# Retention attention and top-1 experts on one core: where the table read, found rows, decayed queries, weight pieces and first loads stand in the program order

## The chip, the cores and the metric

The kernel runs on one core of a Trainium2 chip. The metric is device time in microseconds (us), the median of three runs; three runs of the kernel before took 421.93, 422.62 and 422.92 us, so its time is 422.62 us.

## The reference

Block-wise retention attention (B = 4, H = 8, S = 768, D = 64, blocks of 64) yields x, 3072 rows of 512. A top-1 mixture of 8 experts follows:

```python
logits = x @ w_gate
e_idx = np.argmax(logits, axis=1)
...
for e in range(E):
    mask = e_idx == e
    h = np.maximum(x[mask] @ w1[e], 0.0)
    ye = h @ w2[e]
    out[mask] = gate_w[mask, None] * eom[mask, e, None] * ye
```

Here `gate_w` is the winning probability and `eom` a sigmoid of a second gate. All of it is float32; w1 is 512 x 1024 and w2 is 1024 x 512 for each expert.

## The kernel before, in words

**Attention.** x is made in 24 tiles of 128 rows (`NTILE`). A loop over s = -2 to 21 runs, for each s, `stage_a(s + 2)` (turning keys and queries: psum banks `pk`, `pq`), `stage_c1(s)` (the queries times the running state, into `po`), `stage_b(s + 1)` (keys times queries: `ps`), `stage_b2(s + 1)` (VectorE: `at` = `ps` times the decay table, L396) and `stage_c(s)` (`at` times values, L431, and the copy to `xT`). `decay_queries(n)` (L356) makes the decayed queries `qd` that `stage_c1(n)` reads; for tile 23 the tile is named `qkv_23_1`. `RES` is 16.

**Routing of the first expert ahead of time.** The routes of tiles 0 to 15 (`x_d` holds their rows in DRAM, `store_x` L521) are known before attention ends. `place_scatter` (L697) writes (row, gate) records to the table `tab_d`; `load_rows` (L822) reads an expert's part of it back as `index`; `row_index` (L846, L851) turns that into gather indices `rows`. For expert 0, rows found by a matmul (`pfound`) are added: `row_join` transposes them on VectorE (`found`, L865) and adds (L869). `gather` (L887, GpSimd, an indirect DMA of one 32-row group into `xg`) then fetches rows of x: eight gathers, here called [0] to [7], fill `xg_0_0` and `xg_0_1`, two in each of the steps s = 18 to 21. `pace` (L839, `beat`) makes GpSimd wait for a tile of the attention before the second of each pair. `x_turn(0, 0)` and `x_turn(0, 1)` (VectorE, L904) transpose the two halves into `y_0_0`; `fill` then runs expert 0's first products on TensorE (`ph` from `y` and `raw`, L938) in between the last routing steps. They are the first work of the experts that TensorE can do.

**Experts.** Weights come in 1 MB pieces, four for each expert (`load_piece`, L112, tile `raw`): pieces 0 and 1 are w1 of expert 0, 2 and 3 its w2, 4 and 5 are w1 of expert 1, 6 and 7 its w2. ScalarE and VectorE split each into two parts (`whi`, `wlo`), and a product is three matmuls (L79 to L81); their left side is split into `xhi` (ScalarE, L918) and `xlo` (VectorE, L922). Expert 1's rows are gathered as [0] to [13]: ten behind the read of its indices, the last four during expert 0's second half of rows. `next_split` splits a piece by quarters and loads the one two further on.

**What sets the order.** All of this stands in one hand-written program order (`manual_schedule`): every engine runs its own instructions in that order. SyncE (SP), ScalarE and GpSimd (POOL) issue DMAs, each in its own order. A DMA also waits for the one that stands eight before it among the DMAs of its kind (hardware queues of SP and ScalarE, software queue of POOL), here called its lane. The start loads keys and queries of tiles 0 to 4 and values of 0 to 2 (L200 to L205), then the loop goes on tile by tile; the gate weights `wgs` come over ScalarE's queue at L1237.

Of the kernel before, what the change touches and what calls it, by code (L numbers as in the profile page):

```python
# [23 lines left out]
def kernel(  # L24
# [13 lines left out]
    nc = tc.nc  # L38
# [140 lines left out]
    with tc.manual_schedule():  # L179
# [22 lines left out]
        for n in range(2, AHEAD):  # L202
            load_qkv(n, 0, 2)
            if n > 2:
                load_qkv(n - 2, 2, 3)  # L205
    kdec = const.tile([P, H, 1], F32, name="kdec")
# [151 lines left out]
    def stage_a2(n):  # L358
        c, b = divmod(n, B)
        L = live[n]  # L360
        if c > 0:
            qd = packs[n][3] if n in packs else slot(f"qd_{n}")
            L["qd"] = qd.rearrange("p (g t) -> p g t", g=NPAIR)
            if n not in (RES + 5, RES + 6):
                decay_queries(n)
        weave()
        weave()
        if c < NCH - 1:
            L["kd"] = slot(f"kd_{n}").rearrange("p (h d) -> p h d", h=H)
# [491 lines left out]

    def row_join(j0, pf, width):
        nb = width // 32
        turned = slot(f"found_{j0}")
        nc.vector.transpose(turned[:, 0:width], pf[:, 0:width])  # L865
        gi = const.tile([P, nb], I32, name=f"rows0_{j0}")
# [300 lines left out]
    with tc.manual_schedule():  # L1167
# [12 lines left out]
        for s in range(-2, NTILE - 2):  # L1180
# [19 lines left out]
            if s == RES + 2:  # L1200
                pfound = bank("pfound")
                for b in range(B):
                    found(pfound, RES - B + b, 0, 2 * P, b == 0, b == B - 1)
                row_index(0)
                row_join(0, pfound, 2 * P)
            n = s - 1
# [4 lines left out]
            if n >= 0 and n % B == B - 1:  # L1211
                at_once(route_choose(n + 1 - B, n + 1))
                if n < RES:
                    pace(routed[n + 1 - B][0][0:1, 0, 0:1])
                else:
                    decay_queries(s + 2)
                ranking = route_place(n + 1 - B, n + 1)
                per_turn[0] = 3 if n >= RES - 1 else 2
            stage_k(s + 2)
            if s == RES + 1:  # L1220
# [14 lines left out]
            if s == 1:  # L1235
                weave(len(later))
                nc.scalar.dma_start(wgs[:, :, 0:E], w_gate.rearrange("(c p) e -> p c e", p=P))  # L1237
                nc.scalar.dma_start(wgs[:, :, E : 2 * E], w_output_gate.rearrange("(c p) e -> p c e", p=P))
            if s == 2:
                blank_rows()  # L1240
# [17 lines left out]
            if s >= RES + 2:  # L1258
                pace(xTs[s][0:1, 0:1])
                gather(0, 2 * (s - RES - 2) + 1, 2 * (s - RES - 2) + 2, RES * P)  # L1260
                if s < RES + 4:
                    place_scatter(1)
                if s == RES + 4:
                    load_rows(0, 2, None, nc.gpsimd)
            if s == RES + 5:
                load_piece(1)
            if s < RES:
                place_scatter(1 if s < RES - 2 else 2)

        load_piece(2)  # L1270
        n = NTILE - 1
# [21 lines left out]
        x_turn(0, 1)  # L1293
        stage_d2(n - 3, 2)
        fill(3)
        for f in place[1:]:
# [23 lines left out]
        place_scatter(len(pending))  # L1320
        fill(5)
        row_index(0, 2)
        row_join(2, pfound, late_width)
        gather(0, 8)
# [4 lines left out]
        load_piece(4, nc.gpsimd)  # L1329
        load_piece(5, nc.gpsimd)  # L1330
        load_outs(0)
# [5 lines left out]
        for j in range(4):  # L1337
            split_quarter(3, j)
            if j == 3:
                row_index(1)  # L1340
                gather(1, 0, 10)
            fill(2)
            settle()
# [13 lines left out]

        def next_split(i, quarters):
            for qq in quarters:
                split_quarter(i + qq // 4, qq % 4)  # L1360
                if qq % 4 == 3:
                    load_piece(i + 2 + qq // 4)

        for p in range(E):
# [5 lines left out]
            for fc in range(NFC):  # L1370
                if p == 0:
                    up(p, fc, 1)
                    if fc >= 4:
                        next_split(4, (fc - 4,))
                        for f in work[:2]:
# [211 lines left out]
```

## Time and profile before

| | us |
|---|---|
| three runs | 421.93, 422.62, 422.92 |
| the profiled execution | 423.13 |
| its span in the trace | 421.1 |
| TensorE busy in the span | 401.2 (95%) |
| VectorE busy | 279.1 (66%) |
| ScalarE busy | 183.4 (44%) |
| GpSimd busy | 234.1 (56%) |

The profiled execution is one run by itself; 2.0 us of it lie outside the span that the trace records. The views used are the busy time in windows of the span, the waits of an engine with what released them, the timeline of one engine (start, duration, idle time ahead of it and the releaser), and the view of one source line with the times from issue to landing of its DMAs. A releaser is inferred; where the engine that it names was long done, it was another wait.

### The profile page before, as it was taken

How to read it: one execution, taken by the hardware profiler on the slowest of the kernel's cores; microseconds unless marked ns; L12 is line 12 of the kernel's file. 1: busy time of each engine (PE TensorE's matmuls, PEld its weight loads, DVE VectorE, ACT ScalarE, POOL GpSimd, SP SyncE). 2: the span in 40 equal slices, each digit the busy share in tenths (PEclk: the TensorE clock that was granted, in tenths of full speed). 3: DMA queues.
4: the chain of work that ended last, by engine and by line, in shares of the span. 5: the costliest groups of instructions: out<-in, count | busy, mean ns of one | idle time of the engine just before them, and what ended most of it. 6: DMA issues, size and time to landing. Idle time of an engine off the chain costs nothing.

```text
span 421.1 us, 10323 instructions
## 1 busy us (share of the span) xinstructions
PE 401.2 (95%) x3775; PEld 366.6 (87%) x3775; DVE 279.1 (66%) x789; ACT 183.4 (44%) x449; POOL 234.1 (56%) x306
## 2 busy tenths in 40 slices
PE   7899999998849999999999999999999999999995
PEld 4789889787638898699999999999999989988985
DVE  3858778676847826586778957966885774864511
ACT  3667666685412414445325504704632542551500
POOL 2468876935665768487575557466286356302002
PEclk9999999998979999999999999999999999999999
DMA  9987988999935383355367747936965866462001
GB/s 183 215 200 181 232 226 226 272 269 234 352 121 175 65 318 112 98 196 169 127 189 225 260 161 208 304 132 183 297 211 150 292 237 206 131 188 84 0 26 48
DMA packets 101861, 78.98 MB, mean 188 GB/s; under 512 B 66348, under 2 KB 78128, under 8 KB 101808
## 3 DMA queue, kind: packets, MB, share of 16 engines
q1 hardware_dynamic: 92736, 62.80, 52.2%
q0 software_dynamic: 6816, 15.19, 11.4%
q8 instruction: 31, 0.51, 0.5%
q10 hardware_dynamic: 2256, 0.30, 0.5%
q14 instruction: 22, 0.18, 0.1%
HBM read 62.45 MB, written 16.21 MB: 187 GB/s over the span
## 4 chain that ended last, share of the span: by engine, by line
PE 78%; DMA 9%; DVE 4%; SPq 3%; issue 3%; ACT 1%; POOL 1%; POOLq 0%; ACTq 0%; DVEq 0%
PE ph_None L80 10%; PE ph_None L81 10%; PE ph_None L79 9%; PE py L79 6%; PE py L80 6%; PE py L81 6%; DMA xg<-x_d,rows 5%; PE pyr L81 4%; PE pyr L80 4%; PE pyr L79 4%; PE ph L938 4%; PE ps L387 3%; PE po L431 3%; DMA qkv<-in_q_dram 2%; PE po L411 2%
## 5 line engine op out<-in xcount | busy, mean ns | idle before, releaser
L887 POOL DMA_INDIRECT xg<-x_d,rows x103 | 113.6, 1103 | 65.8 <-issue 30.7
L134 DVE TENSOR_TENSOR wlo<-raw,whi 128x512 fp32r<-128x512 f32 x120 | 79.6, 685 | 0.8 <-ACT whi L125 0.5
L964 ACT ACTIVATE hhi<-ph_None 128x400 fp32r<-128x400 f32 (+4 forms) x56 | 28.0, 501 | 114.4 <-PE ph_None L81 108.2
L79 PE MATMUL ph_None<-xhi,whi 128*128 128x400 f32 (+4 forms) x224 | 76.5, 342 | 0.7 <-ACT xhi L918 0.7
L80 PE MATMUL ph_None<-xlo,whi 128*128 128x400 f32 (+4 forms) x224 | 76.5, 342 | 0.3 <-DVE xlo L922 0.3
L81 PE MATMUL ph_None<-xhi,wlo 128*128 128x400 f32 (+4 forms) x224 | 76.4, 341 | 0.0
L125 ACT CAST whi<-raw 128x512 fp32r<-128x512 f32 x120 | 69.9, 614 | 0.0
L965 DVE SCALAR_TENSOR_TENSOR hlo<-ph_None,hhi 128x400 fp32r<-128x400 f32 (+4 forms) x56 | 31.7, 567 | 34.1 <-ACT hhi L964 33.8
L396 DVE TENSOR_TENSOR at<-ps,decay 128x512 f32<-128x512 f32 x48 | 31.3, 685 | 21.6 <-PE ps L387 21.5
L79 PE MATMUL py<-hhi,whi 128*128 128x400 f32 (+2 forms) x128 | 44.7, 349 | 0.0
L80 PE MATMUL py<-hlo,whi 128*128 128x400 f32 (+2 forms) x128 | 44.7, 349 | 0.0
L81 PE MATMUL py<-hhi,wlo 128*128 128x400 f32 (+2 forms) x128 | 44.6, 349 | 0.0
L79 PEld LDWEIGHTS ph_None<-xhi,whi 128*128 128x128 f32 x224 | 42.1, 188 | 1.5 <-ACT xhi L918 1.2
L80 PEld LDWEIGHTS ph_None<-xlo,whi 128*128 128x128 f32 x224 | 42.1, 188 | 1.0 <-DVE xlo L922 0.6
L81 PEld LDWEIGHTS ph_None<-xhi,wlo 128*128 128x128 f32 x224 | 42.2, 188 | 0.3
L1080 POOL DMA_INDIRECT out_dram<-yn,table x12 | 13.2, 1101 | 49.9 <-DVE yn L1140 32.6
L79 PE MATMUL pyr<-whi,hhi 128*128 128x512 f32 (+2 forms) x96 | 37.8, 394 | 0.0
L80 PE MATMUL pyr<-wlo,hhi 128*128 128x512 f32 (+2 forms) x96 | 37.5, 391 | 0.0
L81 PE MATMUL pyr<-whi,hlo 128*128 128x512 f32 (+2 forms) x96 | 37.5, 390 | 0.0
L347 ACT COPY qT<-pq 64x256 f32<-64x256 f32 x88 | 34.6, 393 | 2.4 <-PE pq L339 1.5
L697 POOL DMA_INDIRECT tab_d<-rec,idx x24 | 24.6, 1023 | 17.1 <-issue 6.5
L938 PE MATMUL ph<-y,raw 128*128 128x256 f32 (+1 forms) x128 | 27.2, 373 | 5.3 <-issue 5.3
(203 smaller groups left out, 715.8 us busy)
## 6 DMA issues: line engine op xcount, KB each, us to landing
raw<-in_moe_w_dram SPq DMA_DIRECT2D x30, 1024.0 KB
x_d<-xn SPq DMA_DIRECT2D x12, 512.0 KB
qkv<-in_k_dram SPq DMA_DIRECT2D x38, 128.0 KB
qkv<-in_v_dram SPq DMA_DIRECT2D x19, 256.0 KB
qkv<-in_q_dram SPq DMA_DIRECT2D x36, 128.0 KB
yd<-yo SPq DMA_DIRECT2D x12, 256.0 KB
yr<-yd SPq DMA_DIRECT2D x48, 64.0 KB
raw<-in_moe_w_dram POOLq DMA_DIRECT2D x2, 1024.0 KB
```

The source lines that it names most:

```text
L79: nc.tensor.matmul(ps, a[0], b[0], start=first, stop=False)
L80: nc.tensor.matmul(ps, a[0], b[1], start=False, stop=False)
L81: nc.tensor.matmul(ps, a[1], b[0], start=False, stop=last)
L125: nc.scalar.copy(out=hi, in_=src)
L134: eng.tensor_tensor(out=lo, in0=src, in1=hi.bitcast(F32), op=ALU.subtract)
L347: copies = [lambda r=r, view=view, src=src: nc.scalar.copy(out=view(qT[r]), in_=src) for r, view, src in query_parts(pq)]
L396: nc.vector.tensor_tensor(out=at, in0=ps.rearrange("p (g t) -> p g t", g=NPAIR), in1=dec[:, j], op=ALU.mult)
L697: nc.gpsimd.indirect_dma_start(out=tab_d, out_offset=bass.IndirectOffsetOnAxis(ap=idx, axis=0), in_=rec, in_offset=None, bounds_check=P * ...
L887: nc.gpsimd.indirect_dma_start(out=xg[(p, b // 4)][:, (b % 4) * P : (b % 4 + 1) * P], out_offset=None, in_=x_q[0 : 4 * rows], in_offset=ba ...
L938: nc.tensor.matmul(phs[(p, fc)][:, r].rearrange("p (b r) -> p b r", b=nb), raws[fc // 4][:, kc, sl], ys[(p, h)][:, 0 : nb * P].rearrange(" ...
L964: nc.scalar.activation(out=hi[:, r], in_=ph[:, r], func=AF.Relu)
L965: nc.vector.scalar_tensor_tensor(out=lo[:, r], in0=ph[:, r], scalar=0.0, in1=hi[:, r].bitcast(F32), op0=ALU.max, op1=ALU.subtract,)
```

## The change

Nine moves, none of which alters an instruction's work:

1. In the first loads, the values of tile 1 go ahead of keys and queries of tile 3 instead of behind them.
2. The two loads of `wgs` go from step s = 1 to s = 2.
3. The decayed queries of tile 23 are made behind `at` of tile 22 instead of ahead of it.
4. At s = 18, the transpose of the found rows is done at once; the part that needs the table read `index_0_0` goes behind `at` of tile 19.
5. The second table read, `index_0_2`, goes from ahead of gathers [6] and [7] to behind them; piece 1 goes from SP's queue to GpSimd's, right behind it.
6. Piece 2 goes behind the store of x tiles 20 and 21 on SP.
7. The transpose of the late found rows goes ahead of the steps that read the second table read.
8. Piece 5 goes, on GpSimd's queue, from right behind piece 4 to behind the first ten gathers of expert 1.
9. Piece 6 goes from SP's queue to GpSimd's, which puts it behind the last four gathers of expert 1.

```diff
--- before.py
+++ after.py
@@ -201,8 +201,8 @@
         load_qkv(0, 2, 3)
         for n in range(2, AHEAD):
             load_qkv(n, 0, 2)
-            if n > 2:
-                load_qkv(n - 2, 2, 3)
+            if n % 2 == 0:
+                load_qkv(n // 2, 2, 3)
     kdec = const.tile([P, H, 1], F32, name="kdec")
 
     lam4 = const.tile([P, NPAIR], F32, name="lam4")
@@ -361,7 +361,7 @@
         if c > 0:
             qd = packs[n][3] if n in packs else slot(f"qd_{n}")
             L["qd"] = qd.rearrange("p (g t) -> p g t", g=NPAIR)
-            if n not in (RES + 5, RES + 6):
+            if n < RES + 5:
                 decay_queries(n)
         weave()
         weave()
@@ -859,10 +859,15 @@
 
     part0 = {}
 
-    def row_join(j0, pf, width):
+    found0 = {}
+
+    def row_turn(j0, pf, width):
+        found0[j0] = slot(f"found_{j0}")
+        nc.vector.transpose(found0[j0][:, 0:width], pf[:, 0:width])
+
+    def row_join(j0, width):
         nb = width // 32
-        turned = slot(f"found_{j0}")
-        nc.vector.transpose(turned[:, 0:width], pf[:, 0:width])
+        turned = found0[j0]
         gi = const.tile([P, nb], I32, name=f"rows0_{j0}")
         for j in range((nb + 3) // 4):
             w = min(4, nb - 4 * j)
@@ -1201,8 +1206,7 @@
                 pfound = bank("pfound")
                 for b in range(B):
                     found(pfound, RES - B + b, 0, 2 * P, b == 0, b == B - 1)
-                row_index(0)
-                row_join(0, pfound, 2 * P)
+                row_turn(0, pfound, 2 * P)
             n = s - 1
             if s >= 1 and s % B == 0:
                 logit_rows(s - B)
@@ -1216,6 +1220,11 @@
                     decay_queries(s + 2)
                 ranking = route_place(n + 1 - B, n + 1)
                 per_turn[0] = 3 if n >= RES - 1 else 2
+            if s == RES + 2:
+                row_index(0)
+                row_join(0, 2 * P)
+            if s == RES + 5:
+                decay_queries(s + 2)
             stage_k(s + 2)
             if s == RES + 1:
                 weave(len(later))
@@ -1234,9 +1243,9 @@
                 order_tables()
             if s == 1:
                 weave(len(later))
+            if s == 2:
                 nc.scalar.dma_start(wgs[:, :, 0:E], w_gate.rearrange("(c p) e -> p c e", p=P))
                 nc.scalar.dma_start(wgs[:, :, E : 2 * E], w_output_gate.rearrange("(c p) e -> p c e", p=P))
-            if s == 2:
                 blank_rows()
             if s == 5:
                 number_tables()
@@ -1260,14 +1269,12 @@
                 gather(0, 2 * (s - RES - 2) + 1, 2 * (s - RES - 2) + 2, RES * P)
                 if s < RES + 4:
                     place_scatter(1)
-                if s == RES + 4:
+                if s == RES + 5:
                     load_rows(0, 2, None, nc.gpsimd)
-            if s == RES + 5:
-                load_piece(1)
+                    load_piece(1, nc.gpsimd)
             if s < RES:
                 place_scatter(1 if s < RES - 2 else 2)
 
-        load_piece(2)
         n = NTILE - 1
         late_width = CAP[0] - 2 * P
         stage_c1(n - 1)
@@ -1292,6 +1299,7 @@
         logits(LAST + 2, 2)
         x_turn(0, 1)
         stage_d2(n - 3, 2)
+        load_piece(2)
         fill(3)
         for f in place[1:]:
             f()
@@ -1319,15 +1327,15 @@
             last[i]()
         place_scatter(len(pending))
         fill(5)
+        row_turn(2, pfound, late_width)
         row_index(0, 2)
-        row_join(2, pfound, late_width)
+        row_join(2, late_width)
         gather(0, 8)
         settle()
         sort_rest(counts)
         expert_regs(1, order_i[:, 1:2], 1)
         load_rows(1)
         load_piece(4, nc.gpsimd)
-        load_piece(5, nc.gpsimd)
         load_outs(0)
         expert_regs(2, order_i[:, 2:E], E - 2)
         for j in range(4):
@@ -1339,6 +1347,7 @@
             if j == 3:
                 row_index(1)
                 gather(1, 0, 10)
+                load_piece(5, nc.gpsimd)
             fill(2)
             settle()
         fill(4)
@@ -1355,11 +1364,11 @@
                 work += [lambda g=g, h=h: x_split(p, g, h) for g in range(NPAIR)]
             return work
 
-        def next_split(i, quarters):
+        def next_split(i, quarters, eng=nc.sync):
             for qq in quarters:
                 split_quarter(i + qq // 4, qq % 4)
                 if qq % 4 == 3:
-                    load_piece(i + 2 + qq // 4)
+                    load_piece(i + 2 + qq // 4, eng)
 
         for p in range(E):
             if p == E - 1:
@@ -1371,7 +1380,7 @@
                 if p == 0:
                     up(p, fc, 1)
                     if fc >= 4:
-                        next_split(4, (fc - 4,))
+                        next_split(4, (fc - 4,), nc.gpsimd)
                         for f in work[:2]:
                             f()
                         work = work[2:]
```

How the instructions stand now, at three places. First VectorE at step s = 18, around the found rows of expert 0 (`rowf` and `rows` come from the table read, `rows0` is what the gathers use, `at_19` what the attention waits for). Before:

```order
L455 TENSOR_TENSOR state_0_137<-state_0_137,pst_17_2069 128x256
L846 SCALAR_TENSOR_TENSOR rowf_0_0_2147<-index_0_0_2047 32x8
L851 TENSOR_SCALAR rows_0_0_2149<-rowf_0_0_2147 32x8 x4
L865 STREAM_TRANSPOSE found_0_2154<-pfound_2138 128x256
L869 TENSOR_TENSOR rows0_0_2156<-found_0_2154,rows_0_0_2149 128x4 x2
L396 TENSOR_TENSOR at_19_0_2159<-ps_19_0_2120,decay_101 128x512
L396 TENSOR_TENSOR at_19_1_2161<-ps_19_1_2121,decay_101 128x512
```

After:

```order
L455 TENSOR_TENSOR state_0_137<-state_0_137,pst_17_2069 128x256
L866 STREAM_TRANSPOSE found_0_2147<-pfound_2138 128x256
L396 TENSOR_TENSOR at_19_0_2149<-ps_19_0_2120,decay_101 128x512
L396 TENSOR_TENSOR at_19_1_2151<-ps_19_1_2121,decay_101 128x512
L846 SCALAR_TENSOR_TENSOR rowf_0_0_2153<-index_0_0_2047 32x8
L851 TENSOR_SCALAR rows_0_0_2155<-rowf_0_0_2153 32x8 x4
L874 TENSOR_TENSOR rows0_0_2160<-found_0_2147,rows_0_0_2155 128x4 x2
```

The three groups that need the table read stood ahead of `at_19`; now only the transpose does, and the table's groups stand behind it.

Second, GpSimd from gather [4] on (`xg_0_1`; `beat` is the pacing copy, `rec_16` the records of tiles 16 to 19). Before:

```order
L887 DMA xg_0_1_2373<-x_d_72,rows0_0_2156 128x128
L839 COPY beat_155<-xT_20_2379 1x1
L887 DMA xg_0_1_2373<-x_d_72,rows0_0_2156 128x128
L822 ISA
L822 DMA index_0_2_2396<-tab_d_73 32x8x3
L887 DMA xg_0_1_2373<-x_d_72,rows0_0_2156 128x128
L839 COPY beat_155<-xT_21_2470 1x1
L887 DMA xg_0_1_2373<-x_d_72,rows0_0_2156 128x128
L697 DMA tab_d_73<-rec_16_2358,idx_16_2372 24576x3 x2
```

After:

```order
L892 DMA xg_0_1_2373<-x_d_72,rows0_0_2160 128x128
L839 COPY beat_155<-xT_20_2379 1x1
L892 DMA xg_0_1_2373<-x_d_72,rows0_0_2160 128x128 x2
L839 COPY beat_155<-xT_21_2468 1x1
L892 DMA xg_0_1_2373<-x_d_72,rows0_0_2160 128x128
L822 ISA
L822 DMA index_0_2_2483<-tab_d_73 32x8x3
L112 ISA
L112 DMA raw_1_2485<-in_moe_w1_dram 128x4x512
L697 DMA tab_d_73<-rec_16_2358,idx_16_2372 24576x3 x2
```

The read of `index_0_2` stood between gathers [5] and [6]; now it stands behind [7], with the load of piece 1 (`raw_1`) behind it and both ahead of the next scatters.

Third, GpSimd at expert 1 (`xg_1_0` to `xg_1_3` are its gathers [0] to [13], L1080 and L1085 the scatters of output rows). Before:

```order
L112 DMA raw_4_2815<-in_moe_w1_dram 128x4x512
L112 ISA
L112 DMA raw_5_2817<-in_moe_w1_dram 128x4x512
L887 DMA xg_1_0_2950<-x_d_72,rows_1_0_2945 128x128 x4
L887 DMA xg_1_1_2963<-x_d_72,rows_1_0_2945 128x128 x4
L887 DMA xg_1_2_2976<-x_d_72,rows_1_0_2945 128x128 x2
L1080 DMA out_0_dram<-yn_0_0_2989,table_0_0_2819 3072x512
L1080 DMA out_0_dram<-yn_0_1_3022,table_0_0_2819 3072x512
L839 COPY beat_155<-hhi_0_0_2723 1x1
L887 DMA xg_1_2_2976<-x_d_72,rows_1_0_2945 128x128 x2
L839 COPY beat_155<-hhi_0_1_2727 1x1
L887 DMA xg_1_3_3053<-x_d_72,rows_1_0_2945 128x128 x2
```

After:

```order
L892 DMA xg_1_1_2961<-x_d_72,rows_1_0_2943 128x128 x4
L892 DMA xg_1_2_2974<-x_d_72,rows_1_0_2943 128x128 x2
L112 ISA
L112 DMA raw_5_2981<-in_moe_w1_dram 128x4x512
L1085 DMA out_0_dram<-yn_0_0_2989,table_0_0_2817 3072x512
L1085 DMA out_0_dram<-yn_0_1_3022,table_0_0_2817 3072x512
L839 COPY beat_155<-hhi_0_0_2723 1x1
L892 DMA xg_1_2_2974<-x_d_72,rows_1_0_2943 128x128 x2
L839 COPY beat_155<-hhi_0_1_2727 1x1
L892 DMA xg_1_3_3053<-x_d_72,rows_1_0_2943 128x128 x2
L112 ISA
L112 DMA raw_6_3131<-in_moe_w2_dram 128x4x512
```

Piece 5 (`raw_5`) stood ahead of all gathers; now it stands behind the first ten. Piece 6 (`raw_6`, before on SP) follows the last four.

## Rows read from the trace of the kernel before

**Rows 1.** Windows: length, busy us (instructions) by engine, TensorE clock, DMA share, GB/s

```profile
95.00:100.00 5.00, 3.54 (x52) 3.03 (x54) 3.93 (x12) 2.59 (x9) 3.31 (x3) 0.71 1.25 272
...
115.00:120.00 5.00, 2.82 (x60) 2.01 (x52) 2.26 (x10) 1.48 (x6) 1.89 (x3) 1.00 0.66 238
120.00:125.00 5.00, 1.45 (x4) 1.21 (x5) 2.23 (x7) 0.00 (x0) 3.86 (x5) 0.60 0.11 28
125.00:130.00 5.00, 5.00 (x24) 4.01 (x23) 3.65 (x18) 1.07 (x4) 4.03 (x8) 0.72 0.32 107
...
200.00:300.00 100.00, 100.00 (x543) 99.35 (x542) 76.09 (x223) 40.60 (x90) 59.53 (x67) 1.00 0.65 202
```

**Rows 2.** TensorE's waits: line, what released it, us in total, times, longest

```profile
PE ph L938 <- issue: 5.3, 1, 5.3
...
PE pq L339 <- DMA q<-in_q_dram: 0.8, 1, 0.8
```

**Rows 3.** Timeline, VectorE: start, us, operation, [idle time before and releaser]

```profile
94.51 0.16 DVE L846 SCALAR_TENSOR_TENSOR rowf<-index 32x8 f32<-32x8 int32 x1 [1.80 <-DMA index<-tab_d]
```

**Rows 4.** Timeline of TensorE at 96 and at 112

```profile
96.02 0.44 PE L411 MATMUL po<-qd,state 64*64 64x128 f32 x4 [1.11 <-DVE found L865]
...
112.46 1.09 PE L387 MATMUL ps<-qT,kT 64*64 64x128 f32 x28 [1.37 <-DVE at L396]
```

**Rows 5.** Timeline of GpSimd, first gather [0], and from gather [5] to gather [7]

```profile
102.75 1.09 POOL L887 DMA_INDIRECT xg<-x_d,rows  x1 [3.71 <-DVE qd L356]
...
112.75 1.02 POOL L887 DMA_INDIRECT xg<-x_d,rows  x1 [0.16 <-issue]
117.71 0.65 POOL L822 DMA_DIRECT2D index<-tab_d  x1 [3.93 <-DMA tab_d<-rec,idx]
118.67 1.06 POOL L887 DMA_INDIRECT xg<-x_d,rows  x1 [0.30 <-ACT lT L483]
...
120.07 1.02 POOL L887 DMA_INDIRECT xg<-x_d,rows  x1 [0.16 <-issue]
```

**Rows 6.** Timeline of VectorE, transpose of the second half of the gathered rows

```profile
122.73 0.71 DVE L904 STREAM_TRANSPOSE y<-xg 128x512 f32<-128x512 f32 x1 [5.29 <-DMA xg<-x_d,rows]
```

**Rows 7.** Timeline of TensorE around the first expert work

```profile
117.64 0.65 PE L479 MATMUL pl<-xT,wgs 128*32 128x128 f32 x16
123.55 2.90 PE L938 MATMUL ph<-y,raw 128*128 128x256 f32 x6 [5.26 <-issue]
...
133.85 1.49 PE L938 MATMUL ph<-y,raw 128*128 128x256 f32 x6
```

**Rows 8.** Line L887, the 103 gathers: durations; issue to landing

```profile
L887 POOL DMA_INDIRECT xg<-x_d,rows x103: 991/1037/1512, 102.7 to 361.5; - x103
...
DMA to landing us min/median/max: 2.6/4.2/6.6
```

**Rows 9.** Timeline of SP, pieces 1 and 2 as issued

```profile
109.19 1.31 SPq L112 DMA_DIRECT2D raw<-in_moe_w_dram  x2
```

**Rows 10.** Timeline of GpSimd, pieces 4 and 5, then three of expert 1's gathers

```profile
144.52 1.66 POOL L112 DMA_DIRECT2D raw<-in_moe_w_dram  x2
...
158.07 1.01 POOL L887 DMA_INDIRECT xg<-x_d,rows  x1 [2.13 <-DMA xg<-x_d,rows]
159.38 1.01 POOL L887 DMA_INDIRECT xg<-x_d,rows  x1 [0.30 <-issue]
...
169.79 1.00 POOL L887 DMA_INDIRECT xg<-x_d,rows  x1 [0.31 <-issue]
```

**Rows 11.** Timeline of VectorE, transposes of expert 1's last gathered rows

```profile
172.88 1.04 DVE L904 STREAM_TRANSPOSE y<-xg 128x512 f32<-128x512 f32 x2 [7.35 <-DMA xg<-x_d,rows]
```

**Rows 12.** Timeline of TensorE, end of expert 0 and start of expert 1

```profile
173.29 0.40 PE L81 MATMUL pyr<-whi,hlo 128*64 128x512 f32 x1
174.36 0.46 PE L79 MATMUL ph_None<-xhi,whi 128*128 128x432 f32 x1 [0.68 <-ACT xhi L918]
175.15 0.46 PE L80 MATMUL ph_None<-xlo,whi 128*128 128x432 f32 x1 [0.33 <-DVE xlo L922]
```

## The prediction

> **What bounds the kernel now.** I read the windows of the span first [rows 1]: from 200 to 300 us TensorE is busy 100.00 of 100.00 at full clock. Whatever arrives earlier at that stretch arrives earlier at the end, and a gain on another engine inside it is worth nothing. So the time can only move where TensorE still idles, and its list of waits names the places [rows 2]: the largest is 5.3 us, once, ahead of the first expert product `ph`. The windows show the same hole: TensorE busy 2.82 of 5 from 115 to 120 and 1.45 of 5 from 120 to 125, where the mean granted clock is 0.60, then 5.00 at 0.72 from 125 to 130: the work behind the hole starts at the lower of the two levels (1.2 GHz) [rows 1].
>
> What ends the hole? TensorE is done with the logits at 117.64 + 0.65 = 118.29 and starts `ph` at 123.55 [rows 7]. The waits say "issue", but VectorE's timeline has the reason: the transpose of the second half of the gathered rows starts at 122.73 after 5.29 us of waiting for a gather [rows 6]. GpSimd's timeline says why that gather is late: gather [5] starts at 112.75, then the engine waits 3.93 us until the table's scatters have landed, issues the read of `index_0_2` at 117.71, and only then [6] at 118.67 and [7] at 120.07 [rows 5]. Gathers [6] and [7] don't use that read; they stand behind it in order. The chain is thus: scatter landed, table read, [6], [7], landing 122.73 - 120.07 = 2.66 us, transpose, 0.82 us later `ph`.
>
> A second, smaller hole stands at the start of expert 1 [rows 12]: the last product of expert 0 starts at 173.29, and the next two at 174.36 and 175.15. At the pitch of the full stretch, 100.00 us by 543 products or 0.18 us [rows 1], they would have stood at 173.47 and 173.66: about 1.5 us are lost. The reason is again a gather: `y_1_1` is transposed at 172.88 after a wait of 7.35 us [rows 11], 3.1 us behind the last gather at 169.79 [rows 10].
>
> **The change part by part.** *Move 5, the table read (the main term).* With the read behind them, [6] follows [5] at the pitch of two gathers in a row, 159.38 - 158.07 = 1.31 us [rows 10], so at 112.75 + 1.31 = 114.06. [7] has the pacing copy ahead of it, pitch 120.07 - 118.67 = 1.40 [rows 5]: 115.46 instead of 120.07, **4.6 us earlier**. If it lands in the same 2.66 us, the transpose runs at 118.1 and `ph` at 118.9. TensorE is free at 118.3 at the latest, so it still waits some 0.6 us, or 2.0 where move 3 takes the 1.37 out of its way. All 4.6 us pass on: the routing steps, scatters and late gathers behind are issued from the same rows and products. The landing is the term with two ends: 2.6 to 6.6 us over the gathers, median 4.2 [rows 8]. I take 2.66, the row of this very gather, since pieces 1 and 2, which SP issued at 109.19 [rows 9], no longer share the DMA engines with it; with the median the gain is 3.1, with the longest 0.7.
>
> Here the Trainium skill speaks against the direction: "SBUF — State Buffer", section "SBUF: two separate sides", says that a DMA issued by GpSimd is starved of descriptors while VectorE runs an operation in its two-port mode, and gathers [6] and [7] now fall among the attention's last products on VectorE. The trace doesn't show it so far: all 103 gathers take 991 to 1512 ns, median 1037 [rows 8]. Two gathers at the slowest of these would cost 2 x (1.51 - 1.04) = 0.9 us.
>
> *Piece 1 on GpSimd's queue.* It is issued behind [7] and the read, at 115.46 + 1.06 + 0.3 + 0.65 = 117.5 to 118.3, some 8 us later than now (109.19). Its issue costs GpSimd 0.83 us (two pieces in 1.66 [rows 10]) ahead of the scatters. Its first use is the third of the six records that start at 133.85 [rows 7], about 134.3, hence 129.7 after the shift. That leaves about 11.8 us of flight; with fewer bytes about than now I cost it at nothing. What it costs without this cover is a rival below. Piece 2, in move 6, goes behind a store on SP; it feeds the second product, which follows all uses of piece 1, so its cover is longer: nothing, with the same bound.
>
> *Moves 3, 4 and 7 (VectorE).* Move 4 takes VectorE's wait of 1.80 us for the table read at 94.51 [rows 3] out from ahead of `at_19`, and with it TensorE's 1.11 at 96.02 [rows 4]. Move 3 takes a part of TensorE's 1.37 at 112.46 [rows 4]. Neither is on the path: the first gather starts at 102.75 [rows 5], over 6 us after its indices were ready. The row's releaser (VectorE's `qd`) can't be its condition, since a gather reads no `qd`; the store of the rows of tiles 14 and 15 is what it reads, and that isn't moved. From [0] to [5] GpSimd then goes at its own pitch. So TensorE only arrives earlier at the wait for [7]. I take 0; the bounds are 0.7 gain, if the attention drags the pacing copies along, and 0.5 loss, if the found rows behind `at_19` come late. Move 7 puts a transpose ahead of a wait: 0 to 0.2 us.
>
> *Moves 1 and 2 (start).* 0.25 MB of values go ahead of 0.5 MB of keys and queries; the bytes ahead of tile 4 stay the same, and so do those of `wgs`. TensorE can win a little there and lose a little, but it meets the query stream again: it waits 0.8 us for queries near 80 us [rows 2]. That wait swallows a gain and covers a loss of up to 0.8. I take 0, bounds -0.3 to +0.3.
>
> *Moves 8 and 9 (expert 1).* Now pieces 4 and 5 are issued in 1.66 us at 144.52, and the gather at 158.07 waited 2.13 us [rows 10]. It is the eighth behind piece 5, so its lane waited for that megabyte. With piece 5 behind [9] the wait goes, and its issue of 0.83 us stands ahead of the last four: they come 2.13 - 0.83 = 1.3 us earlier, against everything else. Of the 1.5 us that are lost at the start of expert 1, **1.3** come back. The bounds are 0 (the last four wait for the pacing copies or another lane) and 1.5. Piece 6 on GpSimd is issued behind [13], near 169.79 - 5.9 + 1.0 = 164.9, some 3.8 us ahead of the end of expert 0 (173.29 - 4.6 = 168.7 for its last product). It holds expert 1's second weights, not its first, so it has the first product as cover: 0, with a bound of 1 us loss.
>
> **The sum.** 4.6 + 1.3 = 5.9 us off the profiled execution's own 423.13: 417.2. That execution lies 0.5 above the median of its three runs (422.62), so the median should be **416.7**.
>
> **The rivals.** *Late landing, the wait only moves.* [6] and [7] now fly while the records of tiles 12 to 15 and the store of tiles 18 and 19 are in flight; the 3.93 us for which the table read waited [rows 5] show how long transfers lasted there. At the median landing the time is 416.7 + 1.5 = 418.2, at the longest 420.6; I take 419.4. For it: the crowd. Against it: two megabytes fewer. Chance 0.24.
>
> *The clock stays up.* After the wait of 1.37 us at 112.46 the clock was still 1.00 in 115 to 120, after 1.11 at 96.02 and a shorter one it was 0.71 over 95 to 100 [rows 1, 4]. The new wait of 0.6 to 2.0 us stands between the two. In the old hole the low clock cost 1.45 x 0.5 = 0.7 us up to 125 and 5.00 x 0.28 = 1.4 us up to 130 [rows 1]; six records took 2.90 us there and 1.49 later [rows 7]. If it doesn't fall, up to 2.1 us more are won: 414.6. Chance 0.16.
>
> *Starved gathers.* A VectorE operation that holds GpSimd's descriptors back would stretch [6] and [7] to the slowest gather seen: 0.9 us, 417.6. That is the rule of the Trainium skill above. Chance 0.03, since the spread of [rows 8] doesn't show it.
>
> *Slower: piece 1 late in GpSimd's queue.* Scatters, late gathers and piece 1 now share one software queue, and TensorE needs piece 1 by 129.7. The longest flight the trace has for a piece there is piece 5's, from 145.4 to the wait's end at 158.07, 12.7 us [rows 10]: by that, 0.9 us are lost and 417.6 remains. The gain is gone when the flight lasts 11.8 + 5.9 = 17.7 us; at 19 the time is 424. The Trainium skill's "DMA: Bandwidth & Descriptors", section "SWDGE vs HWDGE vs iDMA", has only one software queue allocated, and each DMA engine takes turns between it and the hardware queues; no row here shows how the turns are taken. Chance 0.08, as it needs one and a half times the longest flight seen.
>
> *It doesn't do what it says.* If the transpose waits for the end of the crowd, not for the issue of [7], or a lane holds [6] until the old time, the shift is under 0.8 us: 422.5. Chance 0.06.
>
> **How the numbers follow.** The forecast has 0.43, the rivals in order 0.24, 0.16, 0.03, 0.08 and 0.06. A measurement of this kernel can tell about 0.2%, or 0.85 us, from no change. Faster by more: 0.43 + 0.24 + 0.16 + 0.03 = 0.86; within: 0.06; slower: 0.08. The range goes from 413.8 (high clock, with 0.7 of moves 3 and 4) to 420.6 (longest landing) and leaves out the last two and little else.
>
> **What would show it.** Right: [6] near 114.1 and [7] near 115.5, with the read behind; `ph` near 119; TensorE's wait ahead of it under 2 us; no wait of GpSimd ahead of expert 1's [7], and no gap at expert 1's first two products; a hundred full microseconds as now. The clock from 120 to 130 tells the second rival from the forecast. Wrong: the transpose of the second half still waits well beyond 118 with [7] in time (late landing); [6] still near 118 (no effect); a wait of TensorE inside `ph` for piece 1, or scatters behind it that land late (slower); a new wait at expert 1 for pieces 5 or 6.

## The result and the profile after

The changed kernel takes 419.09 us (median of 14 runs, 416.37 to 421.01), the kernel before 422.77 beside it (14 runs, 420.77 to 428.04): a ratio of 0.9912, 95% interval 0.989 to 0.9934. It is 3.7 us faster; 416.7 was forecast, in a range from 413.8 to 420.6. Its profiled execution took 419.80 us, with a span of 418.2. Eight of the runs reported below were taken on a chip (here "the first chip") on which the kernel before itself took anything from 426 to 444 us, so their times decide nothing about differences of 1 to 4 us.

GpSimd's timeline of the changed kernel, the rows that answer to [rows 5], with the gathers [0], [3], [5], [6] and [7], the read of `index_0_2` and piece 1:

```profile
103.67 1.09 POOL L892 DMA_INDIRECT xg<-x_d,rows  x1 [4.87 <-PE po L431]
...
109.65 1.03 POOL L892 DMA_INDIRECT xg<-x_d,rows  x1 [0.16 <-issue]
...
114.13 1.03 POOL L892 DMA_INDIRECT xg<-x_d,rows  x1 [0.16 <-issue]
115.46 1.01 POOL L892 DMA_INDIRECT xg<-x_d,rows  x1 [0.30 <-issue]
...
116.81 1.02 POOL L892 DMA_INDIRECT xg<-x_d,rows  x1 [0.16 <-issue]
117.83 0.67 POOL L822 DMA_DIRECT2D index<-tab_d  x1
118.48 0.84 POOL L112 DMA_DIRECT2D raw<-in_moe_w_dram  x1
```

The wait of 3.93 us ahead of the read is gone. [6] follows [5] at 1.33 us, [7] follows [6] at 1.35; 1.31 and 1.40 were forecast. But the whole chain starts 0.92 us later than before (103.67 against 102.75). VectorE's transposes of the two halves and TensorE (the answers to [rows 6, 7]):

```profile
116.09 0.71 DVE L909 STREAM_TRANSPOSE y<-xg 128x512 f32<-128x512 f32 x1 [4.56 <-DMA xg<-x_d,rows]
...
119.32 0.71 DVE L909 STREAM_TRANSPOSE y<-xg 128x512 f32<-128x512 f32 x1 [1.35 <-DMA xg<-x_d,rows]
```

```profile
111.59 1.09 PE L431 MATMUL po<-at,qkv 128*64 128x128 f32 x16
118.02 0.17 PE L618 MATMUL pr<-oh,tri 128*128 128x16 bf16 x1 [5.33 <-DVE oh L581]
...
118.17 1.08 PE L479 MATMUL pl<-xT,wgs 128*32 128x128 f32 x16
120.13 2.90 PE L943 MATMUL ph<-y,raw 128*128 128x256 f32 x6 [0.88 <-PE pl L479]
...
123.04 4.17 PE L943 MATMUL ph<-y,raw 128*128 128x256 f32 x12
```

The second half lands 119.32 - 116.81 = 2.51 us behind [7], where 2.66 was taken. The first expert product starts at 120.13 instead of 123.55: 3.42 us earlier. TensorE started the last product group of attention (`po`) at 111.59, in the kernel before at 115.93:

```profile
115.93 1.09 PE L431 MATMUL po<-at,qkv 128*64 128x128 f32 x16
```

It won nothing by these 4.34 us: it waits 5.33 us for the routing product (`pr`), as VectorE has to transpose the first half ahead of that choice, and gather [3], issued at 109.65, is there only at 116.09. TensorE's waits ahead of `ph` are 5.33 + 0.88 = 6.21 us, in the kernel before 0.46 ahead of `pr` and 5.26. The windows (length, busy time by engine as in [rows 1], clock, DMA share, GB/s) of the changed kernel:

```profile
110.00:115.00 5.00, 2.69 (x55) 1.89 (x50) 1.53 (x5) 1.60 (x5) 4.25 (x7) 1.00 0.70 247
115.00:120.00 5.00, 1.24 (x19) 0.72 (x18) 2.38 (x9) 0.67 (x3) 3.86 (x6) 0.57 0.19 47
120.00:125.00 5.00, 4.87 (x12) 3.90 (x13) 4.02 (x23) 0.56 (x3) 3.53 (x5) 0.50 0.96 329
125.00:130.00 5.00, 5.00 (x28) 4.16 (x28) 3.69 (x17) 0.90 (x3) 3.42 (x7) 0.91 1.05 295
```

The clock is lower for longer than before: 0.57, 0.50 and 0.91 from 115 to 130, against 1.00, 0.60 and 0.72 [rows 1]. The second batch of twelve products takes 4.17 us; in the kernel before it is this row of TensorE's timeline:

```profile
126.45 3.42 PE L938 MATMUL ph<-y,raw 128*128 128x256 f32 x12
```

So of the 3.42 us that came in, 4.17 - 3.42 = 0.75 went at once. That the longer wait is the reason isn't shown: over five executions the same twelve products took 3.42 us (before), 4.17 (changed), and 3.40, 3.89 and 3.89 in the repeated runs of experiments 1, 2 and 3, where TensorE's two waits ahead of `ph` add up to 5.72, 6.21, 6.63, 8.74 and 3.89 us. The length of the wait doesn't order them. The start of expert 1 (the answer to [rows 10 to 12]; GpSimd, VectorE, TensorE):

```profile
165.61 1.00 POOL L892 DMA_INDIRECT xg<-x_d,rows  x1 [0.30 <-issue]
166.61 0.81 POOL L112 DMA_DIRECT2D raw<-in_moe_w_dram  x1
```

```profile
169.88 0.71 DVE L909 STREAM_TRANSPOSE y<-xg 128x512 f32<-128x512 f32 x1 [7.00 <-DMA xg<-x_d,rows]
170.96 0.45 DVE L909 STREAM_TRANSPOSE y<-xg 128x256 f32<-128x256 f32 x1 [0.37 <-DMA xg<-x_d,rows]
```

```profile
170.63 0.40 PE L81 MATMUL pyr<-whi,hlo 128*64 128x512 f32 x1
171.84 0.46 PE L79 MATMUL ph_None<-xhi,whi 128*128 128x432 f32 x1 [0.81 <-ACT xhi L923]
172.63 0.47 PE L80 MATMUL ph_None<-xlo,whi 128*128 128x432 f32 x1 [0.33 <-DVE xlo L927]
```

No gather waits for piece 5's lane any more, and the last one stands 170.63 - 165.61 = 5.02 us ahead of expert 0's last product instead of 173.29 - 169.79 = 3.50. The transpose that waits for it starts 170.96 - 165.61 = 5.35 us after its issue. In the kernel before the corresponding one is the second in the row of [rows 11], which ends at 172.88 + 1.04 = 173.92; at 0.45 us of its own it started at about 173.5, some 3.7 us behind the issue. The gap is as wide as before: 171.84 - 170.63 = 1.21 us against 1.07. Expert 1 starts 174.36 - 171.84 = 2.52 us earlier. The rest of the span passes that on (246.4 us from there to its end, 246.7 before).

### The profile page after: what moved, and what is told of

It is laid out like the page before. It is cut to its first block, busy times and chain, and to the rows that moved or that the text cites. A ratio compares the mean times of both kernels' runs of the same rounds, so it can differ in the third digit from the quotient of the medians.

```text
span 418.2 us, 10324 instructions
## 1 busy us (share of the span) xinstructions
PE 400.1 (96%) x3775; PEld 365.5 (87%) x3775; DVE 278.8 (67%) x789; ACT 184.3 (44%) x449; POOL 237.0 (57%) x308
## 4 chain that ended last, share of the span: by engine, by line
PE 82%; DMA 8%; SPq 3%; DVE 2%; POOL 2%; issue 1%; ACT 0%; ACTq 0%; POOLq 0%; DVEq 0%
PE ph_None L80 10%; PE ph_None L81 10%; PE ph_None L79 10%; PE py L81 6%; PE py L79 6%; PE py L80 6%; PE ph L943 6%; PE pyr L80 4%; PE pyr L79 4%; PE pyr L81 4%; PE po L431 4%; PE ps L387 3%; DMA xg<-x_d,rows 3%; DMA qkv<-in_k_dram 2%; PE pk L339 2%; PE po L411 2%
## 5 line engine op out<-in xcount | busy, mean ns | idle before, releaser
L1085 POOL DMA_INDIRECT out_dram<-yn,table x12 | 13.0, 1087 | 49.9 <-DVE yn L1145 32.6
L909 DVE STREAM_TRANSPOSE y<-xg 128x512 f32<-128x512 f32 (+2 forms) x29 | 18.3, 642 | 18.1 <-DMA xg<-x_d,rows 17.9
```

## The experiments

**How the runs are read.** The kernel before took 425.45 us beside the repeated runs of experiments 1 and 2 and 422.23 beside experiment 3 and the repeated run of experiment 9. Gather [0] starts anywhere from 100.9 to 105.4 us from one execution to the next. So I read the stages from gather [0] on. "Landing of [7]" is the time from its start to the start of the transpose that waits for it, "expert 1" its first product. All times in us, from one profiled execution each; the ratios are those of the runs:

| kernel | [0] | [7] after [0] | landing of [7] | `ph` after [0] | expert 1 after [0] | ratio to before, interval |
|---|---|---|---|---|---|---|
| before | 102.75 | 17.32 | 2.66 | 20.80 | 71.61 | 1 |
| changed | 103.67 | 13.14 | 2.51 | 16.46 | 68.17 | 0.9912 (0.9890 to 0.9934) |
| read moved alone | 104.34 | 12.94 | 5.58 | 19.33 | 70.71 | 0.9987 (0.9952 to 1.0022) |
| changed, read not moved | 105.36 | 15.53 | 2.72 | 19.07 | 70.07 | 0.9972 (0.9939 to 1.0006) |
| moves 5 and 6 alone | 100.91 | 13.13 | 2.53 | 16.48 | 67.73 | 0.9912 (0.9883 to 0.9940) |
| changed, TensorE kept busy | 103.02 | 12.67 | 2.49 | 15.92 | 65.82 | 0.9894 (0.9860 to 0.9928) |

In the column of `ph` the executions fall into two groups: 15.92 to 16.48 where read and pieces are moved, 19.07 to 20.80 where they aren't, or only the read is.

**Experiment 1, the read moved alone.** In the kernel before:

```diff
-                if s == RES + 4:
-                    load_rows(0, 2, None, nc.gpsimd)
             if s == RES + 5:
+                load_rows(0, 2, None, nc.gpsimd)
                 load_piece(1)
```

> The kernel before with one edit: the second table read goes behind gathers [6] and [7]; piece 1 stays on SP. Theory (the read's place is the gain): the first expert product starts 3 to 4.6 us earlier than in the kernel before, near 119 to 120.5, and the time falls to 418.5 to 420. Rival (the gain comes from the attention's end, which the VectorE moves bring forward): the product starts at 122.5 or later and the time stays within 1 us of 422.8.

On the first chip: 439.29 beside 436.25; it decides nothing. Run again:

> The same kernel as in the first experiment (the kernel before with the second table read behind gathers [6] and [7]; piece 1 stays on SP), run again beside the kernel before, since that run was disturbed. Theory: the read's place alone carries most of the gain. Gathers [6] and [7] start near 114 and 115.5, TensorE is free for the first expert product at about 118.3, and the time is 3 to 4 us under that of the kernel before beside it. Rival: the gain needs the VectorE moves, which let TensorE come to the end of attention earlier; then the time is within 1 us.

424.22 beside 425.45, ratio 0.9987: no gain that can be told from none. My theory fell; the rival's number came out, but experiment 3 refutes its cause. GpSimd did what the theory said, counted from [0], and VectorE shows where the gain went:

```profile
117.28 1.02 POOL L887 DMA_INDIRECT xg<-x_d,rows  x1 [0.16 <-issue]
```

```profile
117.25 0.71 DVE L904 STREAM_TRANSPOSE y<-xg 128x512 f32<-128x512 f32 x1 [2.37 <-DMA xg<-x_d,rows]
...
122.86 0.71 DVE L904 STREAM_TRANSPOSE y<-xg 128x512 f32<-128x512 f32 x1 [3.73 <-DMA xg<-x_d,rows]
```

```profile
108.45 2.06 SPq L112 DMA_DIRECT2D raw<-in_moe_w_dram  x2
```

```profile
115.00:117.00 2.00, 1.25 (x17) 0.98 (x18) 0.00 (x0) 0.74 (x2) 1.70 (x3) 1.00 1.05 380
117.00:119.00 2.00, 0.00 (x0) 0.00 (x0) 1.57 (x7) 0.22 (x1) 1.41 (x3) 1.00 1.08 388
```

[7] starts at 117.28, but lands 5.58 us later. Pieces 1 and 2 were issued on SP at 108.45, and the DMA engines are full from 115 to 119 (share 1.05 and 1.08, 380 and 388 GB/s). In the changed kernel, where pieces 1 and 2 come later, the windows 113 to 119 carry 115, 49 and 68 GB/s:

```profile
113.00:115.00 2.00, 0.00 (x0) 0.00 (x0) 0.00 (x0) 0.11 (x1) 1.83 (x3) 1.00 0.33 115
115.00:117.00 2.00, 0.00 (x0) 0.00 (x0) 0.88 (x3) 0.06 (x1) 1.53 (x4) 0.66 0.19 49
117.00:119.00 2.00, 0.98 (x19) 0.72 (x18) 0.83 (x5) 0.34 (x2) 2.00 (x3) 0.50 0.25 68
```

**Experiment 2, the changed kernel with the read not moved** (piece 1 on SP again):

```diff
-                if s == RES + 5:
-                    load_rows(0, 2, None, nc.gpsimd)
-                    load_piece(1, nc.gpsimd)
+                if s == RES + 4:
+                    load_rows(0, 2, None, nc.gpsimd)
+            if s == RES + 5:
+                load_piece(1)
```

> The changed kernel with the second table read back ahead of gathers [6] and [7], and piece 1 back on SP; all other moves stay. Theory (the read's place is the gain): the wait of some 4 us ahead of [6] is back and the time rises to 422 to 423. Rival (the VectorE moves and the pieces of expert 1 carry it): it stays at 419 to 420.5.

On the first chip: 436.27 beside 436.25; it decides nothing. Run again:

> The same kernel as in the second experiment (the changed kernel with the second table read ahead of gathers [6] and [7] and piece 1 on SP), run again beside the kernel before. Theory: without the read's move the other moves are worth nothing, as gather [7] starts near 120 again; the time is within 1 us of the kernel before. Rival: the other moves keep 2 us or more of the gain.

424.24 beside 425.45, ratio 0.9972: 1.2 us under the kernel before, between the two expectations (within 1 us, or 2 and more), and not to be told from no gain. The interval's lower end, 0.9939, would leave only a third of the gain to move 5, so this run alone doesn't settle the share. The wait ahead of the read is back, shorter, and [7] starts at 120.89:

```profile
118.52 0.66 POOL L822 DMA_DIRECT2D index<-tab_d  x1 [1.89 <-DMA tab_d<-rec,idx]
...
120.89 1.02 POOL L892 DMA_INDIRECT xg<-x_d,rows  x1 [0.16 <-issue]
```

**Experiment 3, moves 5 and 6 alone.** The kernel before, with the read behind [7], piece 1 behind it on GpSimd's queue, and piece 2 behind the store of tiles 20 and 21:

```diff
-                if s == RES + 4:
+                if s == RES + 5:
                     load_rows(0, 2, None, nc.gpsimd)
-            if s == RES + 5:
-                load_piece(1)
+                    load_piece(1, nc.gpsimd)
...
-        load_piece(2)
         n = NTILE - 1
...
         stage_d2(n - 3, 2)
+        load_piece(2)
```

> The kernel before with moves 5 and 6 alone: the second table read behind gathers [6] and [7], piece 1 behind it on the software queue, piece 2 behind the store of tiles 20 and 21. With the read's move alone, gather [7] left near 117.3 but landed 5.6 us later, beside pieces 1 and 2. Theory (the read and the two pieces together are the gain): [7] lands in 2.5 to 3 us, the first expert product starts at 120 to 121, and the time is 2.5 to 4 us under that of the kernel before beside it, ratio 0.9905 to 0.994. Rival (the VectorE moves or the pieces of expert 1 are needed as well): ratio 0.996 or more.

418.08 beside 422.23, ratio 0.9912: the whole gain of the change. VectorE and TensorE:

```profile
116.57 0.71 DVE L904 STREAM_TRANSPOSE y<-xg 128x512 f32<-128x512 f32 x1 [2.82 <-DMA xg<-x_d,rows]
```

```profile
113.81 0.17 PE L618 MATMUL pr<-oh,tri 128*128 128x16 bf16 x1 [1.10 <-DVE oh L581]
...
117.39 2.90 PE L938 MATMUL ph<-y,raw 128*128 128x256 f32 x6 [2.79 <-issue]
...
120.29 3.89 PE L938 MATMUL ph<-y,raw 128*128 128x256 f32 x12
```

[7], at 114.04, lands in 2.53 us, as expected; `ph` stands at 117.39, ahead of the 120 to 121 expected, because this execution's gather [0] starts at 100.91 already. From gather [0] to `ph` it takes 16.48 us, the changed kernel 16.46. Without the VectorE moves TensorE waits 1.10 and 2.79 us here instead of 5.33 and 0.88, and `ph` stands at the same place. So moves 1 to 4 and 7 to 9 together bring nothing that these runs can tell from nothing; by the two intervals of 0.9912 a difference of about 1.5 us either way could hide (an estimate). Experiments 1 and 3 differ only in the two pieces, and the landing of [7] falls from 5.58 to 2.53 us: that is the pieces' part. No run moved both pieces without the read or one piece alone with it, so which of the two matters stays open.

**Experiments 4 and 5, the VectorE moves alone and the start alone.** The kernel before with moves 3 and 4, and with moves 1 and 2. The first was meant to have move 7 too, as its expectation says, but its late transpose (`row_turn(2, ...)`) still stands behind `row_index(0, 2)`, so move 7 was not tested by itself. The main parts of the two edits:

```diff
-            if n not in (RES + 5, RES + 6):
+            if n < RES + 5:
...
-                row_index(0)
-                row_join(0, pfound, 2 * P)
+                row_turn(0, pfound, 2 * P)
...
+            if s == RES + 2:
+                row_index(0)
+                row_join(0, 2 * P)
+            if s == RES + 5:
+                decay_queries(s + 2)
```

```diff
-            if n > 2:
-                load_qkv(n - 2, 2, 3)
+            if n % 2 == 0:
+                load_qkv(n // 2, 2, 3)
```

> The kernel before with moves 3, 4 and 7 alone (decayed queries of tile 23, found rows, late found rows on VectorE). Theory: TensorE comes to the end of attention some 5 us earlier, and waits just that much longer for the gathers; the first expert product starts within 1 us of 123.55 and the time is 422 to 423.3. Rival: what TensorE wins there is kept, and the time is 418 to 420.

> The kernel before with moves 1 and 2 alone (values of tile 1 earlier, gate weights later). Theory: whatever TensorE wins or loses in the first 30 us is gone at the query wait near 80 us: 422.4 to 423.2. Rival: the start's gain passes on, 421.5 or less.

Both on the first chip: 435.91 and 434.10 beside 436.25, intervals 0.9935 to 1.0193 and 0.9742 to 1.0216. They decide nothing by themselves; experiment 3 bounds the two together.

**Experiments 6 and 7, the pieces of expert 1.** The changed kernel with moves 8 and 9 undone (the whole edit below), and with move 9 alone undone (its last two lines):

```diff
         load_piece(4, nc.gpsimd)
+        load_piece(5, nc.gpsimd)
...
-                load_piece(5, nc.gpsimd)
...
-                        next_split(4, (fc - 4,), nc.gpsimd)
+                        next_split(4, (fc - 4,))
```

> The changed kernel with moves 8 and 9 undone: piece 5 again right behind piece 4, piece 6 again on SP. By the prediction's term the time rises by 1.3 us to 420.4. Theory from the trace of the changed kernel, where the gap at the start of expert 1 is as wide as before: the moves won nothing, and the time is 418.7 to 419.6.

> The changed kernel with move 9 alone undone: piece 6 is issued on SP as soon as its buffer is free, some 20 us earlier, not behind gather [13]. Theory (the megabyte right behind [13] is what makes that gather land 5.3 us after its issue): it lands in about 3 us, the gap of 1.6 us at the start of expert 1 closes, and the time is 417.6 to 418.2. Rival (piece 7, or the pace of GpSimd, holds the last gathers): the gap stays and the time is 418.8 to 419.5.

Both on the first chip: 434.17 and 435.36 beside 438.24, intervals 0.9885 to 1.0052 and 1.0070 to 1.0204. The second lies wholly above 1 although the median is lower; on that chip neither decides. Experiment 3 bears on the first, since it has pieces 5 and 6 in the old places: its gap at the start of expert 1 is no wider than that of the changed kernel.

```profile
167.60 0.40 PE L81 MATMUL pyr<-whi,hlo 128*64 128x512 f32 x1
168.64 0.46 PE L79 MATMUL ph_None<-xhi,whi 128*128 128x432 f32 x1 [0.65 <-ACT xhi L918]
169.44 0.46 PE L80 MATMUL ph_None<-xlo,whi 128*128 128x432 f32 x1 [0.33 <-DVE xlo L922]
```

168.64 - 167.60 = 1.04 us, and the way from gather [0] to expert 1 is no longer (67.73 against 68.17). The gap varies between executions: 1.07, 1.64 and 1.04 us with the pieces in the old places (before, experiments 1 and 3), 1.21 and 0.78 with moves 8 and 9 (changed, experiment 2), and 2.21 in experiment 9, where TensorE comes earlier. A few tenths for these moves aren't ruled out; 1.3 is not what these rows show. Whether piece 6 on SP would be better stays open.

**Experiment 8, the first half transposed later.** The changed kernel with `x_turn(0, 0)` right ahead of `x_turn(0, 1)`, so that VectorE makes the routing choice first:

```diff
-        x_turn(0, 0)
         place_scatter(B // 2)
...
+        x_turn(0, 0)
         x_turn(0, 1)
```

> The changed kernel with the transpose of the first gathered half moved on VectorE from ahead of the last-but-one routing choice to right ahead of the transpose of the second half. Theory (only the landing of the second half sets the start of the first expert product): TensorE's wait of 5.3 us ahead of the routing product goes, the same wait stands ahead of the first expert product, which starts within 1 us of 120.1, and the time stays at 418.6 to 420. Rival (VectorE's stand behind the first half is what holds the product up): it starts at 119.3 or earlier, and the time is 417.5 to 418.4.

On the first chip: 442.91 beside 438.24, interval 0.9994 to 1.0445. It decides nothing; whether the order matters stays open.

**Experiment 9, TensorE kept busy in the wait.** The changed kernel with products of zeros that nothing reads:

```diff
         stage_c(n)
+        idle = bank("idle_seam")
+        keep_warm(20)
         pace(xTs[n][0:1, 0:1])
...
         logits(LAST + 2, 2)
+        keep_warm(3)
         x_turn(0, 1)
```

> The changed kernel with 23 products of zeros added on TensorE in its wait for the gathered rows: 20 behind the end of attention and 3 behind the last logits; nothing reads them. Theory (the low clock behind the wait costs 1.4 us on the first six products and 1.3 us on the next twelve): the granted clock stays at 1.00 from 115 to 130, and the time falls by 2 to 2.7 us to 416.4 to 417.1. Rival (those products are slow because their data comes late, or the added work comes in the way): 419 or more.

On the first chip: 441.76 beside 438.24, interval 1.0169 to 1.0422. Run again:

> The changed kernel with 23 products of zeros on TensorE in its wait for the gathered rows, run again beside the kernel before, since its first run was disturbed. Theory (the low clock behind the wait costs 1.4 us on the first six products and 1.3 on the next twelve): clock 1.00 from 115 to 130, 2 to 2.7 us less than the changed kernel, ratio to the kernel before 0.984 to 0.987. Rival (the products wait for data, or the added ones come in the way): ratio 0.990 or more.

417.82 beside 422.23, ratio 0.9894. That is between the two expectations, and its interval covers the changed kernel's ratio, so no gain over the changed kernel is shown by the times. It also lies wholly below the first interval of the same edit: the intervals of the first chip can't be relied on. TensorE and its windows:

```profile
112.84 4.58 PE L191 MATMUL idle_seam<-blank 128*128 128x512 bf16 x19 [0.16 <-issue]
...
118.94 1.56 PE L943 MATMUL ph<-y,raw 128*128 128x256 f32 x6
...
120.45 2.76 PE L943 MATMUL ph<-y,raw 128*128 128x256 f32 x12
```

```profile
168.84 0.57 PE L79 MATMUL ph_None<-xhi,whi 128*128 128x432 f32 x1 [1.82 <-ACT xhi L923]
```

```profile
115.00:120.00 5.00, 4.98 (x39) 2.56 (x37) 3.53 (x10) 0.66 (x3) 3.42 (x6) 1.00 0.34 69
120.00:125.00 5.00, 5.00 (x30) 4.31 (x29) 4.66 (x27) 1.18 (x5) 4.16 (x7) 1.00 1.02 384
125.00:130.00 5.00, 5.00 (x34) 4.48 (x33) 3.79 (x23) 0.96 (x4) 3.82 (x7) 1.00 1.06 277
...
168.00:170.00 2.00, 0.94 (x2) 0.55 (x3) 1.90 (x9) 1.56 (x6) 0.53 (x1) 0.76 0.66 258
170.00:172.00 2.00, 2.00 (x7) 1.82 (x7) 2.00 (x5) 1.63 (x4) 1.56 (x2) 0.50 0.12 41
172.00:174.00 2.00, 2.00 (x11) 1.92 (x10) 2.00 (x4) 0.63 (x2) 1.23 (x1) 0.88 0.11 33
```

The first half of the theory holds: the clock stays at 1.00 from 115 to 130, the six products take 1.56 us instead of 2.90 and the next twelve 2.76 instead of 4.17. That is 2.75 us, and expert 1 starts 68.17 - 65.82 = 2.35 us earlier, counted from gather [0]. Then 1.3 us of it are given back. TensorE now comes to expert 1's start before the rows do, waits 1.82 us there instead of 0.81, and the clock falls at that place (0.76, 0.50 and 0.88 from 168 to 174). From expert 1's first product to its tenth it takes 172.59 - 168.84 = 3.75 us, in the changed kernel 174.30 - 171.84 = 2.46; from the first to the end of the span 416.5 - 168.84 = 247.7 us, in the changed kernel 418.2 - 171.84 = 246.4.

## Why the prediction was right, and where its steps were not

**What bounds the kernel, and the mechanism: right.** The gathers behind the table read set the first expert product, and what reaches expert 1's start is passed on to the end. The number is another matter: 3.7 us came of the 6.1 forecast, and 419.09 lies nearer to the 419.4 of the rival "late landing" than to 416.7. The trace, not the time, decides against that rival: [7] landed in 2.51 us. That the range held the result is partly luck, since its upper end was drawn for a late landing and took up other losses.

**The main term, 4.6 us: right in its cause, 2.6 to 4.3 in size.** From gather [0] to `ph` the change saves 20.80 - 16.46 = 4.34 us, and moves 5 and 6 alone 4.32. Of the sum's parts, the pitches behind [5] and the landing (2.51 for 2.66) came out; 0.46 was lost between [0] and [5] (10.46 us, before 10.00). In the profiled execution only 3.42 showed, since its chain began 0.92 us later: the prediction took [0] as fixed, and it lies between 100.9 and 105.4 in six executions. The size rests on the one execution of the kernel before. Against the repeated run of experiment 2, which has the read in its old place, the saving is 19.07 - 16.46 = 2.6 us.

**The choice of the landing: right, and shown.** The reason given was that the two pieces no longer share the DMA engines with [7]. Experiment 1 takes that reason away and gets 5.58 us; experiment 3 gives it back and gets 2.53. The rival "late landing, the wait only moves" is thus what the read's move does by itself; the pieces' moves, which I costed "at nothing", are the condition of the gain.

**The step that failed: TensorE "is free at 118.3 at the latest", "still waits some 0.6 us, or 2.0", and so "All 4.6 us pass on".** TensorE came 4.34 us earlier to the end of attention, its waits add up to 6.21 us, and it was free at 118.17 + 1.08 = 119.25. The prediction considered only the second half's transpose, not what stands behind the first one on VectorE: the routing choice. The clock is low for longer, and the second batch takes 0.75 us more. Moves 3 and 4 were costed at 0, with 0.5 loss as the bound; they free TensorE, and it idles. (Not all of the 4.34 is theirs: against gather [0], the last `po` group starts 13.2 us later in the kernel before, 10.8 and 10.7 in experiments 1 and 3, which have the same VectorE order, and 7.9 to 8.6 with the moves.)

**The clock rival: refuted for this change, its price near enough.** The clock fell; where it is held up, 2.75 us come back in the two batches, and 2.1 was forecast. Of these, 1.3 are lost again at expert 1.

**Expert 1, 1.3 us: wrong, nothing of it came.** The gathers were issued 1.5 us earlier against expert 0's end, as reckoned, but landed later. The prediction took the start of the row of two transposes (3.1 us behind [13]) as the landing of the last gather; the first of the two reads only [8] to [11], so that figure didn't measure [13]. In four executions:

| kernel | piece 7 | [13] | transposes start |
|---|---|---|---|
| changed | 162.91 | 165.61 | 169.88 |
| read not moved | 166.92 | 169.63 | 173.81 |
| moves 5 and 6 alone | 159.87 | 162.57 | 167.03 |
| TensorE kept busy | 158.96 | 163.19 | 167.27 |

The transposes start 6.9 to 8.3 us behind the issue of piece 7 on SP, but 4.1 to 4.5 us behind [13], which is the closer tie. So these rows don't single out piece 7, and piece 6 can't be the whole reason, since experiment 3 has it in the old place. No run moved piece 7: what holds the gathers there stays open. The bound of 0 for this term was in the prediction.

**The sum.** 4.34 by the main move, less 0.92 for the later start, less 0.75 for the second batch at the lower clock, less 0.14 for the gap, is 2.53, against 2.52 us at expert 1's start. The span ends 2.9 us earlier and the execution takes 3.3 less. The medians differ by 3.7; the later start of this one execution can account for the rest.

**The slower rival:** no wait of TensorE for piece 1 appeared in the changed kernel; GpSimd's queue carried it in time.

## What to carry to other kernels

A small gather that is issued earlier need not land earlier while large transfers are in flight: here the read's move alone gave 0.1%, no more than the noise, and with the two weight pieces moved as well 0.9%. When you free an engine in front of a wait, ask which instruction of another engine it will meet next, in that engine's order. And time won ahead of a wait for data can come back at that wait, and again in the clock behind it.

## What the runs showed of the hardware

The TensorE clock fell to its lower level behind a wait of 1.82 us at expert 1's start in the run with the products of zeros (0.50 from 170 to 172), and kept 1.00 (168 to 176) behind 0.81 at the same place in the changed kernel. In the kernel before it kept 1.00 behind 1.37 at 112.46 and fell in the stretch with 1.11 at 96.02 [rows 1, 4]. So the length of one wait doesn't tell what happens; it has to be read from the clock's row behind the wait. Products of zeros held it up (1.00 over 115 to 130).

A small gather in flight beside the two pieces took 5.58 us to land (DMA share 1.05 and 1.08), and 2.49 to 2.72 us in the five executions in which the pieces had landed or came later.

Two more loads of a megabyte on GpSimd's queue (pieces 1 and 6) didn't stretch the gathers there: those of the changed kernel keep the durations of [rows 8].

```profile
L892 POOL DMA_INDIRECT xg<-x_d,rows x103: 992/1030/1523, 103.7 to 358.6; - x103
...
DMA to landing us min/median/max: 2.5/3.4/6.2
```

By these rows (992 to 1523 ns, median 1030) the starved gathers that the prediction names after the Trainium skill's "SBUF — State Buffer", section "SBUF: two separate sides", did not appear here either.
